# Channel attention followed by a GELU MLP: larger first chunks, other idle products, an earlier gate for the weights and a shorter prefetch

## The chip, the cores and the metric

The kernel runs on one core of a Trainium2 chip. The metric is the device time of one execution in microseconds (us). "Span" is the time from the first to the last instruction in a profile; it is some 1.8 us shorter than the device time.

Names used below, with those of the profile: TensorE (PE) does the matrix products (5240 MATMUL in the kernel before), whose results the kernel keeps in PSUM tiles, called banks below; VectorE (DVE) casts and copies, ScalarE (ACT) squares and does GELU; GpSimd (POOL) and Sync (SP) here mostly start DMA transfers (95 of GpSimd's 127 instructions load v, q and k). The profile shows the clock that TensorE was granted, here full (1.00) or half (0.50); a stretch at half clock is called cold.

## The reference

```python
def _attn_ref(q, k, v, tau):                       # B, N, C = 4, 6080, 256
    qn = q / (np.linalg.norm(q, axis=1, keepdims=True) + 1e-06)
    kn = k / (np.linalg.norm(k, axis=1, keepdims=True) + 1e-06)
    s = kn.transpose(0, 2, 1) @ qn / tau           # 256 x 256 for each batch
    ...                                            # softmax over the last axis: a
    return v @ a

def _moe_ref(x, w_in, w_out):                      # x: 24320 x 256, d_ff = 2048
    h = x @ w_in
    ...                                            # g = gelu(h), tanh form
    return g @ w_out
```

The attention matrix of a batch needs all rows of q and k before it can be normalised. After that v, the attention matrix and `w_in` are one product: the kernel multiplies the attention matrix with `w_in` once (`aw`), and each block of 512 rows of v goes through `aw`, GELU and `w_out`.

## The kernel before

Four batches of twelve blocks. While TensorE does the MLP of a batch, the Gram matrix of the next one is slipped in between. Only the first batch has nothing to hide behind. Its q and k are loaded in chunks ("slots" of 128 rows), cast on VectorE, squared on ScalarE and multiplied on TensorE. "Idle products" are meant to keep TensorE's clock up; nobody reads their results.

```python
first_chunks = chunks_of([2, 5, 6, 6, 6, 6, 6, 4, 3, 2, 1], 1)   # 47 slots + 64 rows, these in chunk 1
TAIL, SHARED = 7, 9
...
for n, ch in enumerate(first_chunks):
    ...                                            # cast to qkb (VectorE), squares to sqb (ScalarE)
    if n >= TAIL - 2:
        keep_clock(size)                           # `size` idle products, 128x512
    for s, rows in slots_of(ch):
        gram(G, qkb, s, rows, ...)                 # two products of 256 columns
    ...                                            # column sums: products with one column
    stage_chunk(n + 4)
    if n == n_chunks - 3:                          # the gate: reads chunk n's data on GpSimd
        nc.gpsimd.tensor_copy(gate[:, 0:1], st[0:1, 1, 0, 0:1])
```

Everything that GpSimd issues afterwards stands behind that copy: `w_in`, v of block 1, `w_out`, the first chunk of batch 1, v of block 2 and so on. The blocks of v are turned by DMA transposes that the Sync engine issues (184 DMA_TRANSPOSE in SP's queue). In the loop over blocks:

```python
turn_v(nb + 2)                                     # DMA transposes for the block after the next
load_v(nb + 3)
for i in range(NP):                                # 8 pairs of 128 columns of d_ff
    hp = ...                                       # 4 products, then GELU on ScalarE
    more_aw(1)                                     # first block: one of the remaining products of aw
    ...                                            # second MLP product of the block before
    next(fill, None)                               # one step of the next batch's attention
```

and in `attention_steps`, which is `fill`:

```python
for n in range(10):
    if n % 3 == 0 and n < 9 and (b, n // 3) not in loaded_of:
        load_qk(b, n // 3)
    ...
for n, ch in enumerate(later_chunks):
    load_qk(b, n + 3)
```

## Time and profile before

| | |
|---|---|
| time, median of 4 runs (first pair) | 762.28 us (762.15 to 763.51) |
| span of the profiled run | 760.8 us |
| norms of the first batch start (`r` on ScalarE) | 39.70 us |
| first MLP product (`hp`) | 44.65 us |
| first MLP product of block 2 | 71.86 us, after a wait of 2.1 us |
| last copy out of PSUM starts | 756.61 us |

Read these as the stations of one line: TensorE is the bound from the first MLP product to the end (90% of the chain; its waits after 44 us add up to 2.6 us), so what counts is how late each station is passed. The groups of instructions tell little here: the two MLP products alone add up to 393.3 + 390.6 us, more than TensorE's 737.9, because matmuls overlap in the records, and the change doesn't touch them.

### The profile page before, as it was taken

The page shows a single profiled execution, that of the slowest core. Times are in us where ns is not written, and L with a number is a line of the kernel's source. Part 1 is how long each engine was busy: PE and PEld are TensorE (multiplying, and loading weights), DVE is VectorE, ACT ScalarE, POOL GpSimd, SP SyncE. Part 2 cuts the span into 40 slices and gives each one's busy share as a digit, 9 for nine tenths or more (in the row PEclk, how much of TensorE's full clock was granted, in tenths as well). Part 3 has the DMA queues.
Part 4 walks back from the last instruction along what each step waited for, and adds up shares of the span by engine and source line. Part 5 has one row for each costly group of instructions (what it writes and reads, how often), then busy time and mean ns, then how long its engine had stood idle before and what let it go on. Part 6 is the DMA issues. An engine that isn't in the chain of part 4 may idle for free.

```text
span 760.8 us, 12295 instructions
## 1 busy us (share of the span) xinstructions
PE 737.9 (97%) x5240; PEld 503.1 (66%) x5240; DVE 277.9 (37%) x486; ACT 420.2 (55%) x412; POOL 70.0 (9%) x127
## 2 busy tenths in 40 slices
PE   4798999999999999999999999999999999999997
PEld 2555666667666666667666666666666666666666
DVE  4644354544412454554430445454441010011011
ACT  5674555555456555555555555555545655555552
POOL 0241001001012011001031000100100000000000
PEclk9999999999999999999999999999999999999999
DMA  9999876225129758412539378722512633322111
GB/s 349 351 190 204 126 128 124 70 54 85 42 72 208 140 125 133 102 43 51 114 75 211 78 134 125 123 77 50 82 42 76 100 82 83 68 74 53 41 56 56
DMA packets 80888, 83.59 MB, mean 110 GB/s; under 512 B 55489, under 2 KB 60353, under 8 KB 80833
## 3 DMA queue, kind: packets, MB, share of 16 engines
q0 software_dynamic: 17648, 32.97, 26.7%
q1 hardware_dynamic: 62816, 48.85, 24.3%
q8 instruction: 41, 0.67, 0.4%
q10 hardware_dynamic: 368, 0.98, 0.4%
q14 instruction: 15, 0.11, 0.1%
HBM read 78.91 MB, written 24.90 MB: 136 GB/s over the span
## 4 chain that ended last, share of the span: by engine, by line
PE 90%; issue 4%; DMA 4%; POOL 1%; SPq 0%; DVE 0%; POOLq 0%
PE yp L462 43%; PE hp L534 41%; PE G L140 4%; DMA vT<-vb 2%; DMA vb<-in_v_dram 1%; PE ps L200 1%; DMA win_bf<-in_moe_w_in_dram 1%; SPq L294 0%; POOL win_bf L309 0%; PE cols L152 0%; PE T L178 0%; POOL filler L116 0%; DVE ysb L483 0%; POOL ident masks.py:199 0%; POOL ident_bf L114 0%
## 5 line engine op out<-in xcount | busy, mean ns | idle before, releaser
L538 ACT ACTIVATE g<-hp 128x1024 bf16<-128x1024 f32 (+1 forms) x384 | 389.3, 1014 | 311.6 <-PE hp L534 311.6
L462 PE MATMUL yp<-wout_bf,g 128*128 128x256 bf16 x3040 | 393.3, 273 | 0.0
L534 PE MATMUL hp<-vT,aw 128*128 128x512 bf16 (+1 forms) x1536 | 390.6, 377 | 2.4 <-DMA vT<-vb 2.1
L462 PEld LDWEIGHTS <-g 128*128 128x128 bf16 x3040 | 296.8, 98 | 113.6
L534 PEld LDWEIGHTS <-aw 128*128 128x128 bf16 x1536 | 149.6, 98 | 107.9 <-issue 3.5
L479 DVE COPY ysb<-yp 128x512 f32<-128x512 f32 (+1 forms) x95 | 64.9, 683 | 404.9 <-PE yp L462 398.4
L403 DVE TENSOR_TENSOR acc<-acc,sq 128x512 f32<-128x512 f32 (+1 forms) x141 | 97.6, 692 | 4.8
L140 PE MATMUL G<-qkb 128*128 128x256 bf16 (+1 forms) x384 | 71.7, 288 | 15.7 <-DVE qkb L241 15.7
L402 DVE TENSOR_TENSOR sq<-qkb 128x512 bf16<-128x512 bf16 (+1 forms) x141 | 58.9, 417 | 0.0
L140 PEld LDWEIGHTS <-qkb 128*128 128x128 bf16 (+1 forms) x384 | 38.2, 102 | 25.0 <-DVE qkb L241 17.5
L280 POOL DMA_DIRECT2D vb<-in_v_dram x47 | 25.5, 543 | 133.3 <-DMA vT<-vb 126.6
L209 DVE TENSOR_SCALAR aw<-ps,rsinv 128x512 bf16<-128x512 f32 x30 | 22.4, 750 | 26.0 <-PE ps L200 25.6
L80 POOL DMA_DIRECT2D qkb<-in_q_dram x24 | 13.1, 547 | 161.5 <-PE hp L534 82.3
L246 ACT ACTIVATE sqb<-st 128x3072 bf16<-128x3072 f32 (+5 forms) x10 | 21.0, 2121 | 10.3 <-DMA st<-in_k_dram 10.3
L241 DVE CAST qkb<-st 128x3072 bf16<-128x3072 f32 (+6 forms) x12 | 14.6, 1224 | 15.3 <-DMA st<-in_k_dram 15.3
L200 PE MATMUL ps<-win_bf,eT 128*128 128x512 bf16 x60 | 17.7, 379 | 0.3 <-DVE aw L209 0.3
L413 POOL TENSOR_TENSOR r<-r,half 128x4 f32<-128x4 f32 x3 | 3.1, 1042 | 141.8 <-DVE r L412 141.8
L80 POOL DMA_DIRECT2D qkb<-in_k_dram x24 | 13.1, 546 | 5.2 <-DMA vb<-in_v_dram 2.6
L519 POOL COPY g<-gr 128x1024 bf16<-128x1024 bf16 x2 | 2.1, 1037 | 104.5 <-PE yp L462 104.5
L438 DVE RECIPROCAL den<-den 128x256 f32<-128x256 f32 x6 | 10.5, 1753 | 0.2
L547 POOL COPY gr<-g 128x1024 bf16<-128x1024 bf16 x2 | 2.1, 1034 | 87.6 <-ACT g L538 87.6
L136 PE MATMUL idle<-filler 128*128 128x512 bf16 x28 | 7.5, 385 | 0.0
(60 smaller groups left out, 79.9 us busy)
## 6 DMA issues: line engine op xcount, KB each, us to landing
out_dram<-ysb SPq DMA_DIRECT2D x44, 512.0 KB, 2.9
vb<-in_v_dram POOLq DMA_DIRECT2D x43, 256.0 KB, 8.4
qkb<-in_q_dram POOLq DMA_DIRECT2D x21, 384.0 KB, 6.2
qkb<-in_k_dram POOLq DMA_DIRECT2D x21, 384.0 KB, 7.8
st<-in_q_dram SPq DMA_DIRECT2D x5, 768.0 KB, 9.8
st<-in_k_dram SPq DMA_DIRECT2D x5, 768.0 KB, 11.3
vT<-vb SPq DMA_TRANSPOSE x184, 3.9
out_dram<-ysb SPq DMA_DIRECT2D x4, 384.0 KB, 3.8
```

The lines of the kernel that those rows point to most:

```text
L80: engines[x].dma_start(out=dst[:, x, 0:size, :], in_=src[b, s0 * 128 : (s0 + size) * 128, :].rearrange("(p s) c -> p s c", s=size))
L140: nc.tensor.matmul(G[:, ic, :], lhsT=qk[:rows, 1, s, ic * 128 : ic * 128 + 128], rhs=qk[:rows, 0, s, :], start=first and ic == 0, stop=las ...
L200: nc.tensor.matmul(ps, lhsT=eT[:, jc, ic * 128 : ic * 128 + 128], rhs=win_bf[:, jc, fs * 512 : fs * 512 + 512], start=jc == 0, stop=jc == 1)
L209: nc.vector.tensor_scalar_mul(dst, ps, scale)
L246: nc.scalar.activation(sqb[:rows, :, lo:hi], st[:rows, :, lo:hi], AF.Square)
L280: nc.gpsimd.dma_start(out=t[:, 0:n, :], in_=v_rows[r0 : r0 + n * 128, :].rearrange("(p s) c -> p s c", s=n))
L402: nc.vector.tensor_mul(sq[:rows], flat, flat)
L403: nc.vector.tensor_add(acc[:rows], acc[:rows], sq[:rows])
L462: nc.tensor.matmul(yp[:rows, at, :], lhsT=g[:, fc, s * 128 : s * 128 + rows], rhs=wout_bf[:, fc, :], start=fc == 0, stop=fc == FC - 1)
L479: nc.vector.tensor_copy(ysb[:, s0 : s + 1, :], yp[:, 0 : s + 1 - s0, :])
L534: nc.tensor.matmul(hp[:, j, :cols], lhsT=aw[:, cc, fc * 128 : fc * 128 + 128], rhs=vT[:, cc, :cols], start=cc == 0, stop=cc == 1)
L538: nc.scalar.activation(g[:, 2 * i : 2 * i + 2, :cols], hp[:, :, :cols], AF.Gelu_apprx_tanh)
```

## The change

The intent was to end the opening of the first batch sooner (equal chunks, the 64 odd rows late, idle products early and few at the end), to have the weights there in time (gate one chunk earlier, counted from the end), to keep the queue in front of v's transposes short (two chunks of prefetch), and to save two short waits (other PSUM banks for half of the remaining `aw` products, a second queue for the last output).

```diff
-    first_chunks = chunks_of([2, 5, 6, 6, 6, 6, 6, 4, 3, 2, 1], 1)
-    TAIL, SHARED = 7, 9
+    first_chunks = chunks_of([6, 6, 6, 6, 6, 6, 4, 3, 2, 2], 7)
+    TAIL, SHARED = 6, 8
+    fillers = [0, 0, 5, 5, 5, 5, 3, 2, 1, 0]
...
-        if n >= TAIL - 2:
-            keep_clock(size)
+        keep_clock(fillers[n])
...
-        if n == n_chunks - 3:
+        if n == n_chunks - 4:
...
-    aw_left = [(fs, ic) for fs in range(2, 4) for ic in range(2)]
+    aw_left = [(2, 0, pY, "y"), (2, 1, pY, "y"), (3, 0, pA, "a"), (3, 1, pA, "a")]
...
-            if n % 3 == 0 and n < 9 and (b, n // 3) not in loaded_of:
-                load_qk(b, n // 3)
+            if n % 5 == 0 and (b, n // 5) not in loaded_of:
+                load_qk(b, n // 5)
...
-            load_qk(b, n + 3)
+            load_qk(b, n + 2)
...
-        for lo, row in st["rests"] if s >= n else []:
-            nc.sync.dma_start(out=out[row : row + rest, :], in_=ysb[lo : lo + rest, s, :])
+        for (lo, row), eng in zip(st["rests"] if s >= n else [],
+                                  (nc.sync, nc.scalar if alone else nc.sync)):
+            eng.dma_start(out=out[row : row + rest, :], in_=ysb[lo : lo + rest, s, :])
```

Lines below the changes shift by one or two, so `hp` is L534 before and L536 after, `yp` L462 and L463, the Gram products L140 and L141.

More of the change, by code (lines that the diff above doesn't have):

```diff
@@ L102, in stage_chunk @@
             else:
-                st = staged[n - 2][:, :, first_chunks[n - 2][1] :, :]
-            load_chunk((nc.sync, nc.scalar if n < 2 else nc.sync), st, 0, first_chunks[n])
+                st = staged[n - 2][:, :, first_chunks[n - 2][1] + first_chunks[n - 2][2] :, :]
+            load_chunk((nc.sync, nc.scalar if n < 1 else nc.sync), st, 0, first_chunks[n])
             staged.append(st)
@@ L363, in more_aw @@
             if aw_left:
-                aw_part(eT, rsinv, aw, *aw_left.pop(0))
+                fs, ic, pool, tag = aw_left.pop(0)
+                aw_part(eT, rsinv, aw, fs, ic, ps=pool.tile([128, 512], FP32, tag=tag, name="ps"))
     vT_of[0] = vT0
```

## The prediction

Passages are cut from the prediction and from three expectations below; each cut is marked. The step from 2.6 to 5.1 us, with which the text goes on to 31.5 + 5.1 + 0.6 = 37.2, was the estimate that the laggard's last packets take twice as long beside the weight loads. That half busy is the limit for the clock was the estimate too. The 0.5 for the last output is an estimate from the 1.14 us of issue.

> **What bounds the kernel now.** I read the page's busy shares and chain first, then TensorE's waits, then the opening engine by engine, because the chain says where there is time to be had.
>
> ```profile
> span 760.8 us, 12295 instructions
> PE 737.9 (97%) x5240; PEld 503.1 (66%) x5240; DVE 277.9 (37%) x486; ACT 420.2 (55%) x412; POOL 70.0 (9%) x127
> PE 90%; issue 4%; DMA 4%; POOL 1%; SPq 0%; DVE 0%; POOLq 0%
> ```
>
> TensorE is busy for 737.9 of 760.8 us and makes 90% of the chain. The change takes no useful product away, so only the 22.9 us of idle TensorE and the idle products that lie on the path can be won. The first 80 us, read in stretches of 5 us, hold 61.33 us of TensorE work, so 18.7 of the 22.9 us lie there. After 44 us the waits view (engine, line, releaser; us in total, times, longest) has only this of TensorE:
>
> ```profile
> PE hp L534 <- DMA vT<-vb: 2.1, 1, 2.1
> PE ps L200 <- DVE aw L209: 0.3, 1, 0.3
> PE hp L534 <- ACT g L538: 0.2, 1, 0.2
> ```
>
> So there are three places: the opening, until the column sums of the first batch are complete; one stall of 2.1 us; and the last output. In the opening, the timeline of TensorE:
>
> ```profile
> 25.61 1.48 PE L140 MATMUL G<-qkb 128*128 128x256 bf16 x12 [0.68 <-DVE qkb L241]
> ...
> 30.78 2.74 PE L140 MATMUL G<-qkb 128*128 128x256 bf16 x12 [2.09 <-DVE qkb L241]
> 33.31 0.50 PE L152 MATMUL cols<-ones_bf,pair 128*128 128x1 bf16 x12
> 33.68 1.23 PE L136 MATMUL idle<-filler 128*128 128x512 bf16 x4
> ...
> 71.86 1.02 PE L534 MATMUL hp<-vT,aw 128*128 128x512 bf16 x4 [2.12 <-DMA vT<-vb]
> ```
>
> From 30.78 TensorE runs without a gap until 39.5: the loads are no longer what it waits for. The timelines of VectorE, ScalarE, GpSimd and the Sync queue:
>
> ```profile
> 34.87 0.70 DVE L241 CAST qkb<-st 128x1024 bf16<-128x1024 f32 x1 [0.37 <-DMA st<-in_k_dram]
> ...
> 39.70 0.17 ACT L320 ACTIVATE r<-cols 128x4 f32<-128x4 f32 x1 [2.74 <-PE cols L152]
> ...
> 33.46 0.21 POOL L261 COPY gate<-st 1x1 f32<-1x1 f32 x1 [31.34 <-DMA st<-in_k_dram]
> ...
> 757.06 1.14 SPq L488 DMA_DIRECT2D out_dram<-ysb  x2
> ```
>
> The last data are there at about 35.6 (the packet records end at 35.0, and a wait ends some 0.6 us after its last packet), but the norms start at 39.70. TensorE is behind by a cold stretch (2.74 in place of 1.48 us for twelve products) and by 4+3+2+1 idle products of 0.216 us.
>
> [...]the six-slot chunk before 30.78 came late, TensorE had worked 1.4 us of the 3.4 before, and the clock was granted at 0.66 on average from 30 to 35 us. [...]the transposes of v ran at one small packet per large one between 59 and 68 us, and took 9.6 us to land (median of the first 80 us) against 3.9 us over the run. [...]the stretches from 10 to 25 us move 414 to 420[...]. [...]
>
> **The change part by part.**
>
> Chunks. Ten in place of eleven, equal first ones, remainder rows late. The opening loads are 2 x 6080 x 256 x 4 B = 12.45 MB; from the first packet at 1.8 us at 0.41 MB/us they end at 32.2 us. Before, the engines on average ended at 33.1: the stretch from 5 to 10 us moves 364 GB/s, since small remainder transfers filled the eight transfers in flight. That is 0.9 us of gain. One DMA engine ended at 35.0, because it fetched 16 KB of instructions from 26.2 to 27.3 us and stayed 1.7 to 2.0 us behind. [...]I expect the laggard: last packet at 34.1, without the next part.
>
> Gate. The weight loads wait for chunk 6 of ten. It ends after 40 of 47.5 slots, 10.49 MB, at 27.4 plus 1.8 for the laggard plus 0.6: 29.8, not 33.46. The first weight packet comes 1.9 us after the gate (35.35 before), so at 31.5. From there [...]the 2.6 us that the laggard still has become 5.1. The last chunk is seen at 31.5 + 5.1 + 0.6 = 37.2, or at 35.6 if no engine lags.
>
> Idle products. Five each before chunks 2 to 5, then 3, 2, 1, 0. Early ones run in waits for loads and cost nothing. From the chunk of four slots on, TensorE has about 6.5 us of work in 9 us, so it is no longer behind, and even one cold stretch fits. The norms then start a fixed time after the last data: cast 0.70, product for q's squares 0.42, eight sums 0.2, releases 0.2, together 1.5 us. That is 37.1 to 38.7, against 39.70: a gain of 1.0 to 2.6, taken as 1.5. The 4.95 us from the norms to the first MLP product at 44.65 stay. The weights fit: the first two quarters are needed 3.2 and 4.1 us after the norms, and landed before 41.3 already.
>
> Prefetch of two chunks. In the order of the GpSimd queue one chunk of q and k (1.57 MB as float32) now comes after the transposes of v that block 2 waits for. Before, this chunk was in flight from 65.2 to 70.5, so the queue drains 5.2 us earlier, and about 1.5 more from the start of the stream. The transposes land at about 71.9 - 6.7 = 65.2, and TensorE wants them at 69.7 - 1.5 - 0.3 = 67.9. The stall of 2.1 us goes, with 2.7 us in hand. Later batches have some 25 us between a load and its use, against about 10 to land, so no new wait.
>
> Banks for the remaining weight products: the 0.3 us wait for VectorE goes; the 0.2 us one is ScalarE's own pace and stays. Last output: the second of two transfers is issued beside the first; 1.14 us of issue becomes about 0.6: a gain of 0.5.
>
> Sum: 1.5 + 2.1 + 0.3 + 0.5 = 4.4 us. 762.3 - 4.4 = 757.9 us; the span goes from 760.8 to 756.4.
>
> **The rivals.**
>
> First, the early weights eat the opening. If they hold up the last chunks for longer than I count, the norms start no earlier than now: 1.5 is lost, 759.4. For: [...]the lagging engine decides. Against: before, four idle products and a cold stretch stood behind the data, and 4.1 us of slack have to be eaten.
>
> Second, the clock. With few idle products at the end TensorE waits for two small chunks; [...]the last sums, five idle products and turns run at half speed: up to 1.5 us, so 759.4 too. For: the 41% window before. Against: 60% windows stayed warm before, and I count 60 to 67% here.
>
> Third, the stall moves and does not go. If the transposes are held by the smaller queue as well, TensorE arrives earlier and waits longer, and the gains of the opening vanish into the stall: only 0.5 to 1 is left, about 761.5. Against: they were slow only while the large packets were there, and one whole chunk less is there.
>
> Fourth, all is better: no lagging engine, 2.6 in place of 1.5, so 756.8.
>
> **Range and chances.** The whole idle time of TensorE after the loads' own end is some 9 us, so 2% (15.2 us) is out of reach, and a loss of 15 us would need a new wait in each batch. 755.8 to 760.4 holds all rivals but the third. Runs before spread over 1.4 us. Faster by over 2%: 0.02; within 2%: 0.97; slower: 0.01.
>
> **What would show it.** Right: r at 37.1 to 38.7 with ScalarE's wait ended by column sums whose data had just landed; the gate at 29 to 30; no cold stretch that ends later than 34 us; no TensorE wait for vT over 0.3 us; the two last transfers on two queues. Wrong: the last cast waits beyond 38 us for loads (first rival), products of 0.22 us for 256 columns after 35 us (second), or a wait of hp for vT of 2 us or more (third).

## The result, and the profile after

The changed kernel takes 758.11 us (median of 4 runs, 757.55 to 759.02), against 762.28. The ratio is 0.9943 with a 95% interval of 0.9926 to 0.996.

The page of the changed kernel, head, TensorE's row and the chain by engine:

```profile
span 756.4 us, 12305 instructions
PE 738.3 (98%) x5248; PEld 504.5 (67%) x5248; DVE 278.2 (37%) x484; ACT 419.8 (56%) x411; POOL 70.7 (9%) x127
PE 95%; DMA 3%; ACT 1%; DVE 0%; SPq 0%; issue 0%; DVEq 0%; ACTq 0%
```

TensorE's share of the chain rises from 90 to 95%. Its waits after 40 us, all of them:

```profile
PE hp L536 <- ACT g L540: 0.2, 1, 0.2
```

The wait for vT and the one for VectorE are gone. The timelines of the same run answer to the lines of the prediction (start, duration, engine, line, operation, count; in brackets the idle time before and what ended it):

```profile
29.14 2.25 PE L141 MATMUL G<-qkb 128*128 128x256 bf16 x12 [2.29 <-DVE qkb L242]
31.18 0.50 PE L153 MATMUL cols<-ones_bf,pair 128*128 128x1 bf16 x12
...
38.09 1.24 PE L137 MATMUL idle<-filler 128*128 128x512 bf16 x5
...
67.66 1.03 PE L536 MATMUL hp<-vT,aw 128*128 128x512 bf16 x4
```

```profile
35.46 0.69 DVE L242 CAST qkb<-st 128x1024 bf16<-128x1024 f32 x1 [0.20 <-DMA st<-in_k_dram]
...
38.27 0.17 ACT L320 ACTIVATE r<-cols 128x4 f32<-128x4 f32 x1 [2.19 <-PE cols L153]
...
29.84 0.18 POOL L261 COPY gate<-st 1x1 f32<-1x1 f32 x1 [27.72 <-DMA st<-in_k_dram]
...
752.87 0.51 SPq L490 DMA_DIRECT2D out_dram<-ysb  x1
752.87 0.55 ACTq L490 DMA_DIRECT2D out_dram<-ysb  x1
```

Two things are to be seen. First, there is still a cold stretch: the twelve products at 29.14 take 2.25 us and not 1.48 (the clock record has half clock from 29.68 to 33.09 us), and from there to 38.09 TensorE has no gap. Second, block 2 starts at 67.66 without a wait.

Station by station, the two first profiles differ by 4.4 us:

| station | before | after | gained up to here |
|---|---|---|---|
| first `hp` | 44.65 | 43.19 | 1.46 |
| TensorE wants block 2 (last Gram product + 0.22) | 69.58 | 67.66 | 1.92 |
| block 2 starts | 71.86 | 67.66 | 4.20 |
| last copy | 756.61 | 752.41 | 4.20 |
| end of the span | 760.8 | 756.4 | 4.4 |

So this pair gives 1.46 to the opening, 0.46 to the banks, 2.28 to the stall, nothing to the 685 us of MLP, and 0.2 to the last output. That looks like the prediction's sum term by term. The experiments show that the first and third terms are not what they seem. The other two hold in all 14 profiles: from the first `hp` to the point where TensorE wants block 2 it is 24.92 to 24.93 us in the four without the edit of the banks and 24.47 to 24.48 in the ten with it, and from the last copy to the end 4.1 to 4.2 us in the four without the edit of the last output and 3.8 to 4.0 in the ten with it.

### The profile page after: what moved, and what is told of

Read it like the earlier page. It is cut to its first block, busy times and chain, and to the rows that moved or that the text cites. A ratio compares the mean times of both kernels' runs of the same rounds, so it can differ in the third digit from the quotient of the medians. Undisturbed runs are those within 1.5% of the kernel's fastest.

```text
span 756.4 us, 12305 instructions
## 1 busy us (share of the span) xinstructions
PE 738.3 (98%) x5248; PEld 504.5 (67%) x5248; DVE 278.2 (37%) x484; ACT 419.8 (56%) x411; POOL 70.7 (9%) x127
## 3 DMA queue, kind: packets, MB, share of 16 engines
q1 hardware_dynamic: 62672, 48.98, 24.3%
## 4 chain that ended last, share of the span: by engine, by line
PE 95%; DMA 3%; ACT 1%; DVE 0%; SPq 0%; issue 0%; DVEq 0%; ACTq 0%
PE yp L463 44%; PE hp L536 43%; PE G L141 5%; DMA st<-in_k_dram 3%; PE ps L201 2%; PE cols L153 1%; ACT sqb L247 0%; PE idle L137 0%; PE T L179 0%; DVE qkb L242 0%; SPq L80 0%; ACT g L540 0%; PE ps L345 0%; PE vps L333 0%; DVE Gs L171 0%
## 5 line engine op out<-in xcount | busy, mean ns | idle before, releaser
L463 PE MATMUL yp<-wout_bf,g 128*128 128x256 bf16 x3040 | 393.3, 273 | 0.0
L536 PE MATMUL hp<-vT,aw 128*128 128x512 bf16 (+1 forms) x1536 | 390.5, 377 | 0.2 <-ACT g L540 0.2
L463 PEld LDWEIGHTS <-g 128*128 128x128 bf16 x3040 | 297.5, 98 | 112.9
L536 PEld LDWEIGHTS <-aw 128*128 128x128 bf16 x1536 | 150.0, 98 | 105.3 <-issue 1.1
L141 PE MATMUL G<-qkb 128*128 128x256 bf16 (+1 forms) x384 | 70.7, 285 | 13.6 <-DVE qkb L242 13.6
L141 PEld LDWEIGHTS <-qkb 128*128 128x128 bf16 (+1 forms) x384 | 38.2, 102 | 23.0 <-DVE qkb L242 15.6
L247 ACT ACTIVATE sqb<-st 128x3072 bf16<-128x3072 f32 (+3 forms) x9 | 20.4, 2286 | 11.2 <-DMA st<-in_k_dram 11.2
L242 DVE CAST qkb<-st 128x3072 bf16<-128x3072 f32 (+4 forms) x11 | 14.7, 1345 | 14.9 <-DMA st<-in_k_dram 14.9
L137 PE MATMUL idle<-filler 128*128 128x512 bf16 x32 | 9.2, 408 | 0.0
```

The lines of the kernel that those rows point to most:

```text
L141: nc.tensor.matmul(G[:, ic, :], lhsT=qk[:rows, 1, s, ic * 128 : ic * 128 + 128], rhs=qk[:rows, 0, s, :], start=first and ic == 0, stop=las ...
L247: nc.scalar.activation(sqb[:rows, :, lo:hi], st[:rows, :, lo:hi], AF.Square)
L463: nc.tensor.matmul(yp[:rows, at, :], lhsT=g[:, fc, s * 128 : s * 128 + rows], rhs=wout_bf[:, fc, :], start=fc == 0, stop=fc == FC - 1)
L536: nc.tensor.matmul(hp[:, j, :cols], lhsT=aw[:, cc, fc * 128 : fc * 128 + 128], rhs=vT[:, cc, :cols], start=cc == 0, stop=cc == 1)
```

## The experiments

Theory after the result: the four terms are separate gains, each from its own part of the change, and the idle products beside the last chunks still delay the opening. Rivals: the stall is cured by the earlier gate and not by the prefetch; the idle products are needed for the clock; and the time of the kernel before is set by when v's transposes land, so that its opening does not matter. Medians and ratios:

| run | chip | median us (lowest to highest) | ratio to before (95%) |
|---|---|---|---|
| undo_prefetch | 15 | 759.82 (759.68 to 760.02) | 0.9946 (0.9921 to 0.9971) |
| only_prefetch | 15 | 759.26 (758.81 to 760.75) | 0.9943 (0.9919 to 0.9966) |
| no_tail_idle | 15 | 759.17 (758.95 to 759.40) | 0.9938 (0.9917 to 0.9959) |
| warm_chunk5 | 15 | 759.15 (758.61 to 759.67) | 0.9938 (0.9916 to 0.9960) |
| changed_again | 14 | 758.06 (757.83 to 758.42) | 0.9925 (0.9910 to 0.9940) |
| old_idle | 14 | 757.83 (757.67 to 757.97) | 0.9921 (0.9906 to 0.9936) |
| undo_gate | 14 | 758.20 (757.88 to 758.33) | 0.9925 (0.9910 to 0.9940) |
| spread_idle | 14 | 757.94 (757.27 to 758.10) | 0.9921 (0.9906 to 0.9936) |
| before_again | 15 | 763.87 (762.10 to 765.12) | 0.9999 (0.9979 to 1.0019) |
| before_warm | 15 | 764.44 (763.44 to 766.19) | 1.0004 (0.9985 to 1.0023) |
| prefetch_banks_end | 15 | 758.80 (758.02 to 759.73) | 0.9937 (0.9922 to 0.9952) |
| short_last | 15 | 758.27 (758.17 to 758.31) | 0.9927 (0.9914 to 0.9941) |

On these two chips the kernel before took 764.12, 763.89 and 764.02 us (medians of the three sets of rounds), spread from 762.1 to 765.7, against 762.28 in the first pair; the changed kernel, run again on chip 14 only, took the same as there. All results were correct. Below 1 us only runs of one set are compared, and stations of the profiles (also across chips), not ratios.

### undo_prefetch: the changed kernel with three chunks of prefetch

```diff
-            if n % 5 == 0 and (b, n // 5) not in loaded_of:
-                load_qk(b, n // 5)
+            if n % 3 == 0 and n < 9 and (b, n // 3) not in loaded_of:
+                load_qk(b, n // 3)
-            load_qk(b, n + 2)
+            load_qk(b, n + 3)
```

> The changed kernel with three chunks of prefetch again. Theory (the extra chunk of q and k in front of the transposes of v makes the stall): the transposes of v for block 2 land at about 70 us, TensorE wants them at 67.4, so a wait of hp for vT of 2 to 3 us is back and the time is 2 to 3 us over the changed kernel, about 760.6. Rival (the earlier gate alone cures the stall): no wait, about 758.1, the same as the changed kernel.

Measured: 759.82 us. TensorE's waits after 40 us in its profile:

```profile
PE hp L536 <- DMA vT<-vb: 1.6, 1, 1.6
PE hp L536 <- ACT g L540: 0.2, 1, 0.2
```

The stall is back, 1.6 us long (I had expected 2 to 3), and the time is 1.7 us over the changed kernel's of the first pair (short_last, nearly the same kernel, took 758.27 on this chip: 1.5 us). So the earlier gate and the earlier stream alone don't cure it; the chunk that was moved back in the queue does.

### only_prefetch: the kernel before with two chunks of prefetch

The edit is the reverse of the one above, on the kernel before.

> The kernel before with two chunks of prefetch alone. Theory: the transposes land some 5 us earlier than 71.9, TensorE wants them at 69.6, the wait of 2.1 us is gone, hp first runs at 44.65 as before, time 760.0 (2.3 less than before). Rival (the stall comes from the late weight loads): the wait stays at 2 us, 762.3.

Measured: 759.26 us, 4.9 us less than the median of before of the same rounds, where 2.3 were expected. Its profile, TensorE:

```profile
30.75 1.48 PE L140 MATMUL G<-qkb 128*128 128x256 bf16 x12 [1.83 <-DVE qkb L241]
...
43.21 1.03 PE L534 MATMUL hp<-vT,aw 128*128 128x512 bf16 x4
...
68.14 1.03 PE L534 MATMUL hp<-vT,aw 128*128 128x512 bf16 x4
```

The wait for vT is gone, as the theory says. But there is something that it doesn't say: with the old chunks, the old idle products and the old gate, the first MLP product runs at 43.21, as in the changed kernel (43.19). The twelve products at 30.75 took 1.48 us, so in this profile the clock was full where it was halved in the first profile of before. The opening of the kernel before is as quick as the changed one's when the clock holds. That made the "1.46 us of the opening" suspect.

### no_tail_idle and warm_chunk5: the idle products beside the last chunks

```diff
-    fillers = [0, 0, 5, 5, 5, 5, 3, 2, 1, 0]
+    fillers = [0, 0, 5, 5, 5, 5, 0, 0, 0, 0]     # no_tail_idle
+    fillers = [0, 0, 5, 5, 5, 12, 0, 0, 0, 0]    # warm_chunk5
```

> The changed kernel without the six idle products beside chunks 6 to 8. Theory (in the changed kernel TensorE is still behind the data from 29 to 38 us, and the idle products are on that path): six products of 0.22 us less, r at 37.0 in place of 38.27, until the last cast (35.5 us) sets it; time 1.2 us less, 756.9. Rival (they are needed for the clock): a cold stretch between 33 and 38 us eats it, r at 38 or later, 758 or more.

> As the run without the six late idle products, but with twelve in place of five ahead of chunk 5, where TensorE waits longest for data. Theory: [...]the clock is full from 29 to 33 us (twelve products of 256 columns in 1.48 us, not 2.25), and r comes at 36.9 to 37.0, set by the last data; time 756.8. Rival (twelve are too many: they run into chunk 5's data): the first product of chunk 5 starts later than 29.2, r no earlier than in the run without late idle products.

Measured: 759.17 and 759.15 us, neither faster. In both the first MLP product runs at 43.97, 0.8 us later than in the changed kernel. Here the rival of no_tail_idle holds, in both: the clock falls. (The rival of warm_chunk5 does not: chunk 5 started at 29.12 and its twelve products took 1.48 us.) In the first, two stretches of one window each (start and end, length, then busy us and count of PE, PEld, DVE, ACT and POOL, then the granted clock, the DMA share and GB/s):

```profile
34.07:37.48 3.41, 3.41 (x37) 2.15 (x35) 2.40 (x4) 1.81 (x4) 3.15 (x4) 0.50 1.16 284
37.48:40.90 3.42, 3.42 (x20) 1.93 (x19) 1.40 (x5) 1.66 (x3) 1.06 (x2) 0.50 1.22 207
```

In the second, the window before the drop at 38.11 us, and five idle products after it:

```profile
34.70:38.11 3.41, 2.43 (x44) 1.83 (x43) 2.39 (x4) 1.19 (x3) 2.45 (x3) 1.00 1.14 267
```

```profile
37.86 2.08 PE L137 MATMUL idle<-filler 128*128 128x512 bf16 x5
```

The clock dropped although TensorE's row was busy for 2.43 of 3.41 us, with no gap over 1.0 us. Most of these 44 products are column sums with one column. That they count little for the clock was my guess, and spread_idle below is built on it; a run that changes them alone was not made, so it was not shown.

The traces say a little more. The half-clock stretch is 3.41 us long in the clock record of the changed kernel (29.68 to 33.09) and in the first of before (30.70 to 34.11), and 6.83 us, two of these, in no_tail_idle (from 34.07); a stretch of this length is called a window here. Busy time alone doesn't sort the windows: this one with 2.43 us was followed by a drop, one with 1.43 us (27.25 to 30.67, prefetch_banks_end) was not. What does is left open.

The last data were there only at 35.9 to 36.1 us in both. In warm_chunk5 the clock was full until 38.11, and r came at 38.04, 2.1 us after the last cast started (36.9 to 37.0 had been expected): the data, and not the idle products, set it. What the fall cost lies behind r.

### changed_again: the changed kernel once more

No edit; it is the yardstick for the next three, on the same chip.

> The changed kernel itself once more, on the chip and in the rounds of the next three, as their yardstick. Theory (the kernel before loses 0 to 3.5 us to a clock that drops or not[...], the changed one less): the changed kernel's runs stay within 1.5 us (757.5 to 759), those of before spread over 2 to 4 us (762 to 766). Rival (plain noise of the chip): both spread alike.

Measured: 758.06 us, spread 0.6 us; before spread 3.2 us (762.33 to 765.57) in the same rounds. So in these rounds the spread is the kernel's, not the chip's. (In the first pair both kernels spread alike, before by 1.4 and changed by 1.5 us over four runs, and that stays unexplained.) In this profile the clock stayed full from 18 us on, and TensorE shows a gap that the first one didn't:

```profile
37.12 0.61 PE L141 MATMUL G<-qkb 128*128 128x256 bf16 x4 [0.79 <-DVE qkb L242]
```

So with a full clock it is the last data (cast from 36.01) that set r, at 38.07. With a cold stretch it is TensorE, at 38.27. The two differ by 0.2 us only, but in the cold profile the last cast also started 0.55 us earlier and took 0.69 and not 1.05 us, so what the cold stretch costs by itself is not shown; nor is why the cast took longer.

### old_idle, undo_gate and spread_idle

```diff
-    fillers = [0, 0, 5, 5, 5, 5, 3, 2, 1, 0]
+    fillers = [0, 0, 0, 0, 6, 6, 4, 3, 2, 2]     # old_idle
+    fillers = [0, 0, 5, 5, 5, 12, 1, 3, 0, 4]    # spread_idle
...
-        if n == n_chunks - 4:
+        if n == n_chunks - 3:                    # undo_gate
```

> The changed kernel with the idle products placed by the old rule: none before chunk 4, then 6, 6, 4, 3, 2, 2. Theory: eleven in place of six lie behind chunk 5's data where TensorE has no gap, so r comes 5 x 0.22 = 1.1 us later (39.3), and the time is 1.1 us over the changed kernel in runs of the same clock, 759.2. Rival (the early ones are what counts, for a clock warm at chunk 5): the cold stretch is longer and the loss is over 2 us; or no loss at all if the data set r.

> The changed kernel with the weight loads waiting for chunk 7 in place of chunk 6. Theory (the early weights neither cost nor earn much): the gate passes at about 32.2, not 29.8; the last chunk is seen 0.5 to 1 us earlier, but TensorE sets r, which stays at 38.2; the transposes for block 2 land 1 to 2 us later and TensorE waits 0 to 0.7 us for them; time 0 to 0.7 over the changed kernel. Rival A (early weights hold up the opening): r 0.5 us earlier or more and the time lower. Rival B (the earlier gate took the stall away): a wait of 1.5 us or more for vT.

> Idle products 5, 5, 5, 12, 1, 3, 0, 4 before chunks 2 to 9: as many as fit into the gaps that the run with twelve before chunk 5 showed (0.3 us before chunk 6, 0.7 before chunk 7, 1.0 before chunk 9). Theory[...]: no cold stretch between 29 us and the MLP, r at 37.6 to 38.0, first MLP product at 42.6 to 42.9, time 0.3 to 0.6 us under the changed kernel and every run within 1 us. Rival (the last data come late enough that idle products only delay them): r at 38.3 or later, no gain.

Measured: 757.83, 758.20 and 757.94 us, all within 0.3 us of the changed kernel. In old_idle r comes at 37.97, not at 39.3: the theory missed. Its profile has a full clock from 24.3 us on, so the extra idle products fell into gaps before the last data, and the data set r, which is the last clause of the rival. Where the idle products stand is worth nothing that these runs resolve, as long as some stand beside the last chunks. In undo_gate the gate passes at 32.66 and not 29.84, but the last cast starts at 35.88, no earlier than with early weights (36.01), r comes at 38.29, and GpSimd's wait for the transposes ends at 66.62 and not 66.18. So the early gate neither delays the loads nor saves time; the 0.4 us vanish in the slack before TensorE comes at 67.7. spread_idle kept the clock full, as intended, but r was at 38.06: the last data set it. Its gain of 0.1 us is no gain.

### before_again: the kernel before once more

> The kernel before, once more, for its spread. Theory (the landing of the transposes for block 2 sets the time, whatever the opening does, and a long wait can make the clock drop after it): hp of block 2 starts at 71.5 to 72.5 also in this profile; if the clock was full in the opening, the wait is 3 to 3.7 us and not 2.1; runs over 762 us of span have a cold stretch after 70 us. Rival (the spread is the cold stretch of the opening alone): hp of block 2 starts 1.5 us later or earlier with the opening, and no cold stretch lies after 40 us.

Measured: 763.87 us, spread 3.0 us. This profile (span 761.6) decides about the opening. Its waits after 40 us begin with this line:

```profile
PE hp L534 <- DMA vT<-vb: 3.0, 1, 3.0
```

And its timeline and the stretch around the stall:

```profile
43.03 1.03 PE L534 MATMUL hp<-vT,aw 128*128 128x512 bf16 x4
...
71.07 1.66 PE L534 MATMUL hp<-vT,aw 128*128 128x512 bf16 x4 [2.96 <-DMA vT<-vb]
72.53 1.91 PE L462 MATMUL yp<-wout_bf,g 128*128 128x256 bf16 x8
```

```profile
70.00:75.00 5.00, 3.93 (x15) 1.84 (x16) 2.75 (x6) 1.02 (x1) 0.53 (x1) 0.66 1.11 228
```

The clock was full at chunk 6 this time, and the first MLP product ran at 43.03, 1.62 us earlier than in the first profile of before. It bought nothing in the end. Block 2 started at 71.07, 0.79 us earlier than in the first profile and outside the 71.5 to 72.5 that I had expected; the wait grew to 3.0 us, and after it the clock was down (0.66 on average from 70 to 75 us): eight products that take 1.04 us took 1.91. The chain view of the first profile of before shows what block 2 waits for. From 2.12 us on it has no piece of TensorE's before block 2, so the opening's products are not on it ("issue" is here GpSimd's wait up to the gate, "SPq" are the transposes that Sync issues):

```profile
2.12 31.33 issue
33.67 2.84 POOL win_bf L309 x3
36.51 7.82 DMA win_bf<-in_moe_w_in_dram
44.61 10.91 DMA vb<-in_v_dram
55.53 1.29 SPq L294
...
59.44 12.28 DMA vT<-vb
71.86 1.02 PE hp L534 x4
```

Against changed_again (chip 14, before_again chip 15), station by station:

| from before_again to changed_again | us |
|---|---|
| first `hp` 43.03 to 42.99 | 0.04 |
| banks: TensorE wants block 2 at 67.95 and 67.47 | 0.44 |
| stall: block 2 starts at 71.07 and 67.47 | 3.12 |
| block 2 to the last copy, 686.37 and 684.75 us: the cold stretch after the stall | 1.62 |
| last copy to the end of the span | 0.18 |
| sum (761.6 to 756.2) | 5.40 |

### before_warm: twelve idle products before chunk 6 of the kernel before

```diff
-            keep_clock(size)
+            keep_clock(12 if n == TAIL - 1 else size)
```

> The kernel before with twelve in place of six idle products ahead of its chunk 6, so that the clock is full in the opening. Theory: r at 38.2 in place of 39.7 and the first MLP product at 43.2, but the transposes still land at 71.9: the wait of hp for vT grows from 2.1 to 3.6 us and the time does not fall, 761.5 to 764. Rival (the opening is on the path that sets the end): 1.5 us less in all, 760.8 or under.

Measured: 764.44 us, no gain (ratio 1.0004); the profile is that of its slowest run, 766.19 us. The first MLP product ran at 43.91 in its profile, not 43.2, because the clock rose only at 27 us and the twelve products ended late; still 0.74 us before the 44.65 of the first profile. And again it bought nothing:

```profile
PE hp L534 <- DMA vT<-vb: 4.0, 1, 4.0
```

```profile
70.00:75.00 5.00, 1.97 (x6) 0.84 (x7) 3.63 (x7) 0.01 (x1) 0.53 (x1) 0.64 1.26 185
75.00:80.00 5.00, 5.00 (x26) 2.65 (x25) 0.00 (x0) 2.04 (x2) 1.59 (x3) 0.67 0.80 119
```

A wait of 4.0 us, two cold windows' length after it (0.64 and 0.67 on average over these 10 us, so 6.9 us at half clock), span 764.4. Block 2 started at 73.03, a microsecond later than the theory says, so where exactly the transposes land differs from run to run. What holds in all three profiles of before is that an opening between 43.0 and 44.7 us did not decide when block 2 starts (first `hp` at 43.03, 43.91 and 44.65, block 2 at 71.07, 73.03 and 71.86).

### prefetch_banks_end: without the chunks, the idle products and the gate

The kernel before with the edits of prefetch, banks and last output, as in the change.

> The changed kernel's prefetch, banks and last output with the chunks, idle products and gate of the kernel before. Theory (with a full clock those three are all that the change is worth): runs with a full clock take 758.1 to 758.6, like the changed kernel; runs with a cold stretch at 30 us take 1.5 to 2 us more, which the changed kernel does not. Rival (chunks, idle products and gate are worth over 1 us even with a full clock): no run under 759.

Measured: 758.80 us. Two runs with mean clock 1.0 take 758.02 and 758.80 (the second is over the 758.6 expected); the slowest two 759.51 and 759.73. So three of the six parts give nearly all of the gain. What chunks, idle products and gate add is 0.5 us in the median against short_last on the same chip, and perhaps steadiness: 1.7 us of spread here, 0.1 to 0.8 us in the runs with equal chunks and late idle products on chips 14 and 15, but 1.5 us in the first four runs of the changed kernel. The changed kernel itself was not run on chip 15. The profile of this run had a full clock, so where the slow runs lose their time was not seen.

### short_last: for a version that beats both

```diff
-    first_chunks = chunks_of([6, 6, 6, 6, 6, 6, 4, 3, 2, 2], 7)
+    first_chunks = chunks_of([6, 6, 6, 6, 6, 6, 4, 4, 2, 1], 7)
-    fillers = [0, 0, 5, 5, 5, 5, 3, 2, 1, 0]
+    fillers = [0, 0, 5, 5, 5, 12, 1, 3, 1, 2]
```

> For a version that beats both: chunks 6, 6, 6, 6, 6, 6, 4, 4, 2, 1 and idle products 5, 5, 5, 12, 1, 3, 1, 2 before chunks 2 to 9. Theory (where the last data set r, half as much work behind them is half a microsecond): r at 37.3 to 37.6 against 38.06, time 757.4. Rival (TensorE is behind again because the chunk before is larger): r at 38.0 or later, 757.9 or more.

Measured: 758.27 us, no gain; the rival holds.

```profile
34.56 1.37 PE L141 MATMUL G<-qkb 128*128 128x256 bf16 x10 [1.03 <-DVE qkb L242]
```

The larger chunk 7 came later, TensorE waited 1.03 us for it and had no gap after that; r was at 38.32. No kernel here beats the changed one by more than the runs resolve.

## Why the prediction was right or wrong

The time (757.9 predicted, 758.11 measured) and the span (756.4, 756.4) are right. Some of the steps are not.

**Right: the prefetch.** The transposes were to land at 65.2 with TensorE wanting them at 67.9. GpSimd's wait for them ended at 66.0 and TensorE came at 67.66. Undone alone, the stall came back with 1.6 us; done alone, it went, and none of the ten profiles with two chunks has a wait of TensorE's for vT, so the third rival is out. The edit by itself was worth less than the 5.2 us counted: it moved the end of GpSimd's wait by 3.9 us, done alone (72.28 to 68.39) and undone alone (69.87 against 66.00). The packets show how: in the kernel before 104 to 166 packets of 256 bytes pass in each 2 us from 60 to 68 us, beside large ones, and 1107 from 70 to 72, with few large ones left. The median landing time in the first 80 us, which the prediction quotes, is 9.6 us after the change too, so it doesn't measure this.

**Right in size, wrong in meaning: 1.5 us for the opening.** The step that failed is the sum, which takes the opening and the stall as separate gains. In the kernel before the start of block 2 hung on the transposes: before_again had the quick opening and gained nothing. With a full clock in both openings the change shortens the opening by 0.04 us and the stall by 3.12. The first profile of before happened to have its cold stretch in the opening, so the same loss showed up there as 1.46 + 2.28. In the changed kernel no stall lies behind the opening, so there it counts: in no_tail_idle the first `hp` is 0.78 us later than in the first profile after the change, and the span 0.8 us longer. How close the first profile of before was: in its window ahead of the cold stretch TensorE was busy for 1.40 us, in the same window of prefetch_banks_end for 1.43, and there the clock stayed full.

**Missing: the clock after the stall.** I had priced the stall at its 2.1 us alone. The wait of 3.0 us in before_again was followed by a cold stretch (granted clock 0.66 from 70 to 75 us), and block 2 to the last copy took 1.62 us longer there than in changed_again. The whole gain is therefore more than 4.4 there: 5.4 us between these two profiles, 5.8 by the medians on chip 14. So the total of 4.4 came true in part by luck of the first pair, whose profile of before has the short stall and a full clock after it. "Runs before spread over 1.4 us" rested on four runs: it was over 3 us in the later sets. That the stall's clock makes all of that spread was not shown run by run: the profiles of before_again and before_warm have it (granted clock 0.66 from 70 to 75 us; 0.64 and 0.67 from 70 to 80), the first one of before, with its wait of 2.1 us, does not (1.00 from 65 to 90).

**Wrong: the early weights slow the last chunks by 2.5 us.** The gate passed at 29.84 (29.8 predicted), but by the packet records the first weight packet came at 33.03, when the last chunks were nearly through. (29.8 + 1.9 is 31.7; the prediction's 31.5 is a slip.) The step that was wrong is the 1.9 us from gate to packet: 3.2 here and 3.4 in changed_again, but 1.9 in undo_gate, whose gate passes at 32.66. Why is open. The last data were seen at 35.5 to 36.0, not 37.2, and undo_gate had them at 35.9. The first rival is worth nothing. The lag after the instruction fetch was real, so the fourth rival didn't come true: after the 16 KB (24.8 to 25.9 us) chunk 5 was cast 5.16 us after chunk 4, where the others came 3.8 us apart. In the kernel before and in old_idle the fetch was later (from 26.2 and 27.8 us), and there chunk 6 came late instead. The packet records don't name the DMA engine, so that it is one of sixteen is inferred: in the kernel before, at 28.25 us, 15 packets of 4096 bytes are in flight and one of the 6144 of the chunk before, in the changed kernel, at 26.25, the same.

**Half wrong: TensorE is no longer behind.** That is so with a full clock (gap of 0.79 us in changed_again) and not in the first profile, where it worked without a gap from 29.14 to 38.09. That r was inside the range both times is luck in part: the data came earlier than the 37.2 allowed for, but where they set r it came 2.06 us after the last cast began, not 1.5; the cast alone took 1.05 us and not 0.70.

**Second rival.** The cold stretch came, at chunk 5 and not at the end, and ended at 33.09 (34 had been allowed). Half busy, by which I had judged windows, did not decide: after 1.43 of 3.41 us the clock stayed full (prefetch_banks_end), after 2.43, mostly column sums, it fell (warm_chunk5). The few late idle products, whose worth I had doubted, prevent the other one: without them 0.8 us were lost in the opening.

**Sizes.** With the 64 odd rows late the stretch from 5 to 10 us moves 424 GB/s, where it moved 364. The banks were worth 0.44 to 0.46 and not 0.3: apart from the wait, the products could again start 0.86 us after the four before them, and so overlap. The last output was worth 0.2 and not 0.5: both transfers are issued at 752.87, but the end moved by less than the issue; why was not looked into.

## What to carry to other kernels

Before waits are added up as gains, ask of each whether a later wait would swallow it: an opening in front of a stall that ends at a landing of its own was worth nothing until the stall was gone (first `hp` 1.62 us earlier in before_again, no gain). Many small transfers that someone will soon need can be held up by a large prefetch issued just before them (here the wait for the transposes ended 3.9 us earlier without it); the order in one queue was worth more here than chunk sizes, idle products and an early gate together. And a stall can cost more than its length when the clock falls after it (1.62 us on top of a wait of 3.0 in before_again), which showed here as a spread of the times (over 3 us in the later sets of before) before it showed in one profile.

## What the windows and the instruction fetch show

- Gaps of 2.09 and 2.29 us were followed by a window at half clock. These are four windows of 3.41 us that hold most of such a gap; the first two were followed by the drop (kernel before, changed kernel), the other two were not (only_prefetch, prefetch_banks_end). TensorE was busy for 1.40 and 1.11 us in the first two, for 1.58 and 1.43 in the others, and for 2.43 before the drop in warm_chunk5:

```profile
27.29:30.70 3.41, 1.40 (x10) 0.42 (x6) 1.74 (x2) 1.73 (x1) 0.00 (x0) 1.00 1.02 402
```

```profile
26.27:29.68 3.41, 1.11 (x8) 0.58 (x7) 2.36 (x2) 2.35 (x1) 0.00 (x0) 1.00 1.01 398
```

```profile
27.50:30.91 3.41, 1.58 (x13) 0.60 (x10) 1.98 (x2) 1.96 (x1) 0.00 (x0) 1.00 1.01 400
```

```profile
27.25:30.67 3.42, 1.43 (x11) 0.45 (x7) 1.71 (x2) 1.70 (x1) 0.00 (x0) 1.00 1.02 403
```

- Instruction fetch: no wait of TensorE's for it is seen, but the loads fell behind. With 1.1 us of fetch (16 KB, 26.2 to 27.3 us in the kernel before, 24.8 to 25.9 in the changed one) one chunk of six slots was cast 4.9 to 5.3 us after the one before (5.17 and 5.16 in these two) in place of 3.8, in 13 profiles. In old_idle, where the fetch came 3 us later, it was the next chunk (four slots, 4.16 us).
- A second issuing engine for the last of two transfers of 64 KB saved 0.2 us here.
